# Loading a third block of query weights ahead of a second block of tokens, and spreading the second tokens' layer-norm statistics over ScalarE and VectorE

## The chip, the cores and the metric

The kernel runs on one core of a Trainium2 chip. The metric is device time in microseconds (us) of one execution. Every kernel here was run several times, each time on the same chip next to the kernel before. One execution of each was recorded with the hardware profiler, and its trace is what the readings below come from.

Engines in the profile lines: PE is TensorE's matmuls, PEld its weight loads, DVE is VectorE, ACT is ScalarE, POOL is GpSimd, SP is SyncE. SPq is the queue on which SP issues DMAs. L272 is line 272 of that kernel's source; the lines of the changed kernel are shifted by a few.

## The reference, cut to what matters

A transformer block with adaptive layer norm. Tokens are 2048 x 1024, there are 32 query heads and 4 key/value heads of 128, and attention goes over the last 512 keys.

```python
h = _layernorm(x) * (1 + ca) + sa          # ca, sa from silu(c) @ w_mod
x = x + ga * _A_ref(h, k_cache, v_cache, wq, wo)     # q = h @ wq; softmax attention; @ wo
h = _layernorm(x) * (1 + cb) + sb
x = x + gb * _B_ref(h, w_gate, w_up, w_down)         # SwiGLU feed-forward
```

Only the first layer norm, of the second chunk of 512 tokens (four tiles of 128 tokens, numbered 4 to 7), and the first query projections are touched by the change.

## The kernel before: the parts that matter

A tracker inserts a semaphore wait wherever an operation reads or writes a buffer that another engine has touched. In the traces each engine works through its own operations in the order of emission. This is the second chunk's path from tokens to a matmul operand:

```python
def ln_stats(t):                      # VectorE: two bn_stats halves, one aggregate; POOL: 1/sqrt(var+eps)
    stats(t, t % 2, 0)
    yield
    stats(t, t % 2, 1)
    aggr(t % 8, t % 2)
    yield

def norm_turn(ch, tt):                # VectorE normalises one tile; SP's DMA transposes it into hT
    t = ch * TPC + tt
    norm(t, t % 8, t % 2, half=True)
    T.op(Q_ln[t % 2], lambda: SP.dma_start_transpose(hT[ch % 2][:, :, tt*P:(tt+1)*P], nscf[t % 2]),
         reads=[B_ns4[t % 2]], writes=B_hT[ch % 2])
# later: modulate(...) scales and shifts each of the 8 blocks of hT on VectorE, in place
```

All four transposes name the same eight buffers of `hT` as written, so each waits for the one before to land, and the modulation waits for the last.

The prologue works on the first chunk. Then come attention iterations `i = 1, 2, ...`. In each, PE runs an optional query projection, the scores of iteration i-1, and the product with V (`pv`) of i-2. The relevant emissions of an iteration, before the change:

```python
def pre0(i):
    ...
    if i in (1, 3, 5):
        q_bias_mm(i + 1, i + 3, QB)             # bias of two heads; VectorE copies it out of bank QB
    if i < NQ0 + 1:
        if i % 2 == 0:
            qproj(NQ0 - 1 + i // 2)             # 8 matmuls into bank QB, then VectorE empties the bank
    elif i + 3 < NDI:
        qproj(i + 3)                            # i = 9: projection 12, the first that reads hT[1]
    if i < 5:
        norm_turn(1, i - 1)                     # iterations 1 to 4
    if 1 <= i < 4:
        stats_now(TPC + i)                      # iterations 1 to 3, whole tiles on VectorE
    if i in (7, 8):
        for dt in range(4 * (i - 7), 4 * (i - 7) + 4):
            modulate(hT[1], B_hT[1], dt, 0, 0, B_mode)
```

The statistics of tile 4 are computed on ScalarE at the end of the prologue.

The softmax here doesn't subtract the row's maximum and nothing guards it: scores larger than these inputs give would overflow.

## Time and profile before

| | |
|---|---|
| time, median of the first 3 runs | 1161.9 us (1161.82 to 1164.61) |
| span of the profiled run | 1160.2 us |
| PE busy | 1143.8 us |
| PE busy in 30 to 60 us | 27.2 of 30 us |

The page's first part (per engine: busy us, share of the span, instructions), for the kernel before:

```profile
PE 1143.8 (99%) x7019; PEld 588.7 (51%) x7105; DVE 819.0 (71%) x1641; ACT 530.6 (46%) x741; POOL 68.2 (6%) x136
```

The Trainium skill, "Perfetto Trace Analysis", Identifying the Most-Contended Engine, warns that matmul busy time says little about the distance to the roofline. It is used here for something else: to find where PE stands still. In the stretches of the kernel before (stretch, its length, then for each of PE, PEld, DVE, ACT and POOL the busy us and the instruction count, then granted PE clock, DMA share, GB/s), the third line is nearly full, so what can be won lies before 60 us.

```profile
10.00:15.00 5.00, 4.21 (x47) 3.18 (x46) 2.74 (x9) 1.56 (x4) 0.93 (x3) 0.69 1.09 356
30.00:60.00 30.00, 27.24 (x278) 16.99 (x281) 25.62 (x65) 21.41 (x30) 5.72 (x11) 1.00 0.75 175
60.00:90.00 30.00, 29.69 (x294) 18.66 (x297) 17.97 (x39) 18.84 (x26) 3.14 (x5) 1.00 0.76 164
```

PE's timeline of the kernel before (start, duration, engine, line, operation, count, and in brackets the idle time before it and what released it) shows the gaps:

```profile
31.31 0.81 PE L272 MATMUL ps<-arena 128*128 128x512 bf16 x3 [0.29 <-DVE arena L673]
...
33.74 3.66 PE L272 MATMUL ps<-arena 128*128 128x512 f16 x28 [0.99 <-DVE bq L668]
...
39.77 1.08 PE L272 MATMUL ps<-arena 128*128 128x129 bf16 x16 [0.87 <-DVE arena L821]
...
51.43 12.87 PE L272 MATMUL ps<-arena 128*128 128x512 bf16 x108 [0.24 <-ACT arena L799]
```

(PSUM is the memory that matmuls write to; a bank is a part of it, and it must be emptied before the next matmuls can use it.) The 0.99 us precedes projection 8, whose bank is freed by a bias copy that stands behind eight shifts in VectorE's queue. The 0.87 us precedes the second `pv`, whose banks VectorE empties late because bn_stats stand before that work. Two lines that looked harmless in this profile turn out to matter: POOL's two weight loads, and the last layer-norm transpose on SP's queue shortly after them.

```profile
43.44 1.79 POOL L939 DMA_DIRECT2D arena<-in_A_wo_dram  x2
```

```profile
45.11 1.23 SPq L446 DMA_TRANSPOSE arena<-nsc  x1
```

The 1.23 us is only the issue. The DMA view of the kernel before, asked for 45 to 47 us, gives in its last column the time from issue to landing: 6.2 us, so this transpose landed at about 51.3.

```profile
arena<-nsc SPq DMA_TRANSPOSE x1, 6.2
```

The modulation that reads it, on VectorE, began at 52.39. The transpose had 1.1 us to spare, and nobody waited.

```profile
52.39 1.38 DVE L432 TENSOR_SCALAR arena<-arena,gain,mod_bf 128x512 f16<-128x512 f16 x4
```

The chain that ended last, by engine, in the kernel before:

```profile
PE 95%; DVE 3%; ACT 1%; issue 1%; DMA 1%; SPq 0%; DVEq 0%; ACTq 0%
```

### The profile page before, as it was taken

Reading aid. Unit: us, or ns where it says so; the run is one execution under the profiler, and the core shown is the slowest. Engines: PE = TensorE matmul, PEld = TensorE weight load, DVE = VectorE, ACT = ScalarE, POOL = GpSimd, SP = SyncE. Lnnn points to the kernel's source line nnn. Section 1 sums busy time; section 2 is a strip of 40 time slices with the busy share of each in tenths; the row PEclk is TensorE's granted clock in tenths of the full one; section 3 lists DMA queues with packets and bytes.
Section 4 is the critical chain, followed back from the end, with each engine's and each line's share of the span. In section 5 each row is a group of like instructions: output and inputs, shape, how many; then the busy total and the mean of one; then the engine's idle time right before and its main releaser. Section 6 shows DMA issues by size and latency. Waiting matters only on the chain.

```text
span 1160.2 us, 18184 instructions
## 1 busy us (share of the span) xinstructions
PE 1143.8 (99%) x7019; PEld 588.7 (51%) x7105; DVE 819.0 (71%) x1641; ACT 530.6 (46%) x741; POOL 68.2 (6%) x136
## 2 busy tenths in 40 slices
PE   8999999999999999999999999999999999999999
PEld 5565556554446666566444444444444444444444
DVE  4858997758576777776567898767558777776536
ACT  3766777730117777787110344454110444544110
POOL 1100221000000111111000010000000000000000
PEclk9999999999999999999999999999999999999999
DMA  9779999967906998844765332333764424234443
GB/s 326 170 174 218 221 208 218 211 162 203 248 10 171 193 204 192 213 97 107 193 189 183 76 106 73 101 82 100 208 185 155 123 74 109 73 95 131 131 160 109
DMA packets 289941, 179.98 MB, mean 155 GB/s; under 512 B 130496, under 2 KB 278080, under 8 KB 289856
## 3 DMA queue, kind: packets, MB, share of 16 engines
q1 hardware_dynamic: 226880, 92.31, 36.4%
q10 hardware_dynamic: 54336, 55.05, 14.8%
q0 software_dynamic: 8640, 31.46, 9.3%
q8 instruction: 56, 0.92, 0.3%
q14 instruction: 29, 0.24, 0.1%
HBM read 128.45 MB, written 19.92 MB: 128 GB/s over the span
## 4 chain that ended last, share of the span: by engine, by line
PE 95%; DVE 3%; ACT 1%; issue 1%; DMA 1%; SPq 0%; DVEq 0%; ACTq 0%
PE ps L272 95%; ACT arena L799 1%; DMA arena<-in_A_wq_dram 1%; DVE arena L829 1%; DVE st L413 1%; DVE arena L900 0%; DVE arena L678 0%; SPq L341 0%; DVE arena L673 0%; SPq L310 0%; DVE nsc L427 0%; DVE arena L846 0%; PE ps L276 0%; DVE arena L1544 0%; DVE arena L647 0%
## 5 line engine op out<-in xcount | busy, mean ns | idle before, releaser
L272 PE MATMUL ps<-arena 128*128 128x512 f16 (+2 forms) x6714 | 1135.5, 330 | 12.4 <-POOL arena L406 2.2
L272 PEld LDWEIGHTS ps<-arena 128*128 128x128 bf16 (+1 forms) x6800 | 578.2, 98 | 562.8 <-DVE arena L829 6.2
L799 ACT ACTIVATE arena<-ps 128x1024 bf16<-128x1024 f32 x256 | 261.3, 1021 | 48.4 <-PE ps L272 36.6
L832 ACT ACTIVATE tmp<-ps 128x512 f32<-128x512 f32 x167 | 99.7, 597 | 295.5 <-PE ps L272 282.1
L900 DVE TENSOR_TENSOR arena<-arena 128x512 f16<-128x512 bf16 x328 | 133.4, 419 | 3.0
L829 DVE TENSOR_TENSOR arena<-ps,tmp 128x512 bf16<-128x512 f32 (+1 forms) x134 | 91.9, 686 | 49.7 <-PE ps L272 38.2
L832 ACT ACTIVATE nsc<-ps 128x512 f32<-128x512 f32 x84 | 50.1, 596 | 93.2 <-PE ps L272 90.9
L821 DVE TENSOR_TENSOR arena<-ps,rl 128x512 f16<-128x512 f32 x128 | 88.5, 692 | 4.7 <-DVE rl L818 0.2
L829 DVE TENSOR_TENSOR arena<-ps,nsc 128x512 f16<-128x512 f32 x84 | 57.4, 687 | 40.8 <-PE ps L272 29.6
L818 DVE RECIPROCAL rl<-ps 128x4 f32<-128x4 f32 x128 | 23.1, 180 | 87.8 <-PE ps L272 86.8
L1529 ACT ACTIVATE arena<-arena 128x512 f16<-128x512 f16 x84 | 49.9, 624 | 32.7 <-DVE arena L829 32.7
L1038 DVE TENSOR_TENSOR arena<-arena 128x2048 f16<-128x2048 f16 (+3 forms) x56 | 56.1, 1011 | 9.3 <-PE ps L272 8.8
L1114 DVE TENSOR_TENSOR tmp<-ps,tmp 128x512 f32<-128x512 f32 x32 | 22.1, 690 | 53.1 <-ACT tmp L832 45.3
L832 ACT ACTIVATE arena<-ps 128x512 f32<-128x512 f32 x16 | 9.6, 597 | 90.9 <-PE ps L272 90.9
L950 DVE TENSOR_TENSOR arena<-arena 128x512 f16<-128x512 bf16 x120 | 47.9, 420 | 2.2 <-DMA arena<-in_A_wo_dram 1.2
L413 DVE BATCH_NORM_STATS2 st<-x_res 128x6 f32<-128x512 bf16 x60 | 41.0, 683 | 4.3 <-DMA x_res<-in_A_x_dram 3.9
L427 DVE TENSOR_SCALAR nsc<-x_res,mv,rstd 128x1024 f16<-128x1024 bf16 (+1 forms) x30 | 16.2, 539 | 27.6 <-DMA arena<-nsc 27.6
L1544 DVE TENSOR_TENSOR arena<-arena 128x512 f16<-128x512 f16 x84 | 35.0, 417 | 0.3
L1115 DVE TENSOR_TENSOR tmp<-tmp,rowb 128x512 f32<-128x512 f32 (+1 forms) x49 | 33.6, 686 | 1.7
L594 DVE SCALAR_TENSOR_TENSOR arena<-arena 128x1024 bf16<-128x1024 bf16 x24 | 29.2, 1216 | 0.0
L1116 DVE TENSOR_TENSOR arena<-tmp,x_res 128x512 bf16<-128x512 f32 (+1 forms) x33 | 22.3, 676 | 1.1
L829 DVE TENSOR_TENSOR arena<-ps,rowb 128x512 f16<-128x512 f32 x28 | 19.3, 689 | 3.9 <-ACT rowb L832 3.4
(87 smaller groups left out, 331.5 us busy)
## 6 DMA issues: line engine op xcount, KB each, us to landing
arena<-in_A_wq_dram SPq DMA_DIRECT2D x28, 512.0 KB, 4.9
arena<-wo_sum ACTq DMA_DIRECT2D x7, 2048.0 KB, 9.1
arena<-in_B_w_gate_dram SPq DMA_DIRECT2D x28, 512.0 KB, 4.0
arena<-in_B_w_up_dram SPq DMA_DIRECT2D x28, 512.0 KB, 4.9
arena<-wd_sum ACTq DMA_DIRECT2D x8, 1792.0 KB, 7.9
arena<-in_B_w_down_dram ACTq DMA_DIRECT2D x6, 1792.0 KB, 7.1
arena<-in_A_wo_dram POOLq DMA_DIRECT2D x16, 512.0 KB, 5.0
wo_sum<-arena POOLq DMA_DIRECT2D x16, 512.0 KB, 4.7
```

The costliest lines, as they stand in the source:

```text
L272: T.op(PE, lambda: TE.matmul(out_ap, lhsT, rhs, start=start, stop=stop, skip_group_check=skip), reads=reads, writes=[bank_buf])
L413: T.op(DVE, lambda: V.bn_stats(st_[sl][:, hf * 6:hf * 6 + 6], x_res[:, t, hf * 512:hf * 512 + 512]), reads=[B_x[t]], writes=[B_st[sl]])
L799: T.op(ACT, lambda: A.activation(ex_s[es][:, 2 * kp:2 * kp + 2, :], banks2(SCB + 2 * kp), AF.Exp, scale=att_scale), writes=[PB[SCB + 2 * k ...
L821: T.op(DVE, lambda: V.tensor_tensor(o_s[os_].rearrange("p (a b) d -> p a b d", a=2), psap(PVB * 512, [[512, 2], [130, 2], [1, P]]), rlb, A ...
L829: T.op(DVE, lambda: V.tensor_tensor(out, bank(ba), other, ADD), reads=[ob2], writes=[PB[ba], ob])
L832: T.op(ACT, lambda: A.activation(dst, bank(bk), AF.Copy), writes=[PB[bk], db])
L900: T.op(st, lambda: eng.tensor_tensor(o, a, b, op), reads=rd, writes=[wr])
L950: T.op(DVE, lambda: V.tensor_tensor(o, a, b, SUB), reads=rd, writes=[wr])
L1038: T.op(DVE, lambda: V.tensor_tensor(o, a, b, SUB), reads=rd, writes=[sb])
L1115: T.op(DVE, lambda: V.tensor_tensor(tm, tm, rw, MULT), reads=[B_row[row]], writes=[tb])
L1529: T.op(ACT, lambda: A.activation(o, s_, AF.Silu), reads=[sb], writes=[ob])
L1544: T.op(DVE, lambda: V.tensor_tensor(gu[blk][:, p, :], o, s_, MULT), reads=[sb, ob], writes=[B_gu[blk][p]])
```

## The change

The intent: bring the query weights of projection 8 in before the second tokens; take one more tile's statistics from VectorE, which has no gap from 31.3 to 46.4 us, to ScalarE; cut the rest into half steps, so that no long piece of work delays the emptying of PSUM banks. The normalisations move from iterations 1-4 to 3-6, the modulation from 7-8 to 8-9 and in front of the projection. The diff, cut to its core:

```diff
             load_v(0)
             load_k(1)
+            load_wq(2)
             load_x(1)
-            load_wq(2)
 ...
             def stats_act(t):                    # now a generator in two half steps
-                o, ob = nsc4[t % 2], B_ns4[t % 2]
+                o, ob = tmp[0][:, :].bitcast(BF16), B_tmp[0]
                 T.op(ACT, ... AF.Copy, accum_out=acc[:, 0:1] ...)
                 T.op(POOL, ... mean ...)
+                yield
                 T.op(ACT, ... AF.Square, bias=mean, scale=-1.0, accum_out=acc[:, 1:2] ...)
                 rstd_of(sl, acc[:, 1:2], B_acc, 1.0 / D)
+                yield
 ...
             qproj_mm(7, QB0[7], HK, DT)
-            stats_act(TPC)
             q_raw(7)
 ...
+            x1_stats = [both(stats_act(TPC), stats_act(TPC + 1)), both(ln_stats(TPC + 2), ln_stats(TPC + 3))]
+            NORMS = {3: 0, 4: 2, 5: 1, 6: 3}
 ...
             def pre0(i):
+                if i in (8, 9):
+                    for dt in range(4 * (i - 8), 4 * (i - 8) + 4):
+                        modulate(hT[1], B_hT[1], dt, 0, 0, B_mode)
                 if i < NQ0 + 1:
                     if i % 2 == 0:
                         qproj(NQ0 - 1 + i // 2)
                 elif i + 3 < NDI:
                     qproj(i + 3)
-                if i < 5:
-                    norm_turn(1, i - 1)
-                if 1 <= i < 4:
-                    stats_now(TPC + i)
-                if i in (7, 8):
-                    ... modulate ...
+                if i in NORMS:
+                    norm_turn(1, NORMS[i], i % 2)
+                if 2 <= i < 6:
+                    next(x1_stats[1])
 ...
             def tick0(i):
+                if 1 <= i < 5:
+                    next(x1_stats[0])            # a ScalarE half step behind each exp pair
```

## The prediction

> **What bounds it.** TensorE: the chain that ended last is 95% matmul; the page shows PE busy 1143.8 of 1160.2 us. The change touches the prologue and the first ten attention iterations, 28 to 60 us. The table of stretches gives PE 27.2 of 30 us in 30:60, so at most 2.8 us (0.24%) can be won; 60:90 has 0.3 us idle. PE's gaps in the timeline: 0.29 at 31.3 (VectorE shift of head 0), 0.99 at 33.7 (bias copy, queued behind eight 0.35 us shifts), 0.87 at 39.8 (pv normalisation of iteration 0, queued behind VectorE statistics), 0.24 at 51.4 (ScalarE exp), small ones at 44.7 and 45.3. VectorE has no gap from 31.3 to 46.4.
>
> **What changes.**
> 1. Load order. The second tokens landed at 28.8 and kept ScalarE idle 2.2 us, but no matmul waited for that. The third query weights landed at 31.8 (issue 19.5 plus 12.3); their first matmul ran at 33.7 and waited for VectorE. So the order alone is worth about 0. Tokens will land near 31.5; ScalarE asks for them near 33.8.
> 2. One tile's statistics (1.42 us bn_stats plus aggregate) go from VectorE to ScalarE, which now does two tiles in four half steps, one behind each exp pair of iterations 1 to 4. A half step occupies it 1.15 us (trace: 1.06 and 1.15 us plus a 0.19 us accumulator read, overlapping). The Trainium skill, "ScalarE: Activation LUTs", What ACT_TABLE_LOAD costs, gives 186 ns + 0.833 N (plus 93 ns for a pointer bias): 1.04 and 1.13 us for N = 1024; the trace agrees. No table load is added (instruction order).
> 3. VectorE keeps two tiles, a 0.7 us half in each of iterations 2 to 5; normalisations move from iterations 1-4 to 3-6, modulation of the second chunk from 7-8 to 8-9.
>
> **Critical path, walked by hand with trace durations.** The 0.29 and 0.99 us gaps stay. The 0.87 us gap goes: that normalisation should end near 38.4, not 39.7. New waits: (a) the first normalisation, iteration 3, needs the ScalarE half step that ends near 39.4 plus 1.1 us on POOL, so VectorE idles about 1.3 us near 39.2 to 40.5, and 0.4 us near 46.5; behind it pv waits about 0.5 us near 46. (b) exps come later: ScalarE carries 2.0 + 1.15 us per iteration against 3.3 us of PE. (c) the second half of the modulation (4 x 0.34 us) now stands directly before the projection that reads it, in iteration 9, and behind that iteration's pv normalisation: PE should stop about 0.8 us there (near 58). Sum: -0.9 for the gap, +0.2 to 0.5 for (a) and (b), +0.5 to 1.0 for (c): about 0 to +1 us. After 60 us PE is full, so this stays to the end.
>
> **Predicted**: 1162.5 us (80%: 1160.3 to 1164.6). Faster by over 2%: 0.5%; within 2%: 99%; slower: 0.5%.
>
> **What would show it.** Right: the 0.87 us gap near 39.8 gone; VectorE idle before the norm in iteration 3, released by POOL; no PE wait for query weights in either kernel; a new PE wait released by the modulation near 58; busy PE in 30:60 again 26.5 to 28 us; ScalarE's 2.2 us wait for tokens gone.
>
> **What would make it wrong.** If the transposes of the last normalisation land late (3.7 us median, each waits for the one before), the modulation blocks VectorE and PE by more, +2 us. If the modulation beats the matmuls, the change wins 1 to 1.5 us. If tokens land after 34, everything behind the first half step slips.

## More of the kernel before

After the last of its small `rstd` operations, POOL issues two loads of 512 KB each of the output projection's weights (`unit_load`, first called in iteration 8). Nothing in the program holds them back. They go out as soon as POOL's queue reaches them: in the kernel before that is in iteration 4, four iterations before the place where they stand in the program.

## The result

| | before | changed |
|---|---|---|
| runs | 6 | 6 |
| median | 1163.13 us | 1165.9 us |
| lowest to highest | 1161.82 to 1164.61 | 1164.18 to 1167.36 |
| span of the profiled run | 1160.2 us | 1162.4 us |

The ratio is 1.0023, with a 95% interval of 1.001 to 1.0037. Ratios here are the mean time of one kernel's runs over that of the other's of the same rounds, so not quite the ratio of the medians quoted. The change makes the kernel slower by about 0.2%, or 2.7 us. That is well inside 2%, but 1165.9 us lies above the range of the forecast, and the forecast change was +0.6 us (1162.5 against the 1161.9 then known).

The same stretches of the changed kernel:

```profile
10.00:15.00 5.00, 4.29 (x78) 3.77 (x75) 2.94 (x9) 1.89 (x4) 0.75 (x2) 1.00 1.09 352
30.00:60.00 30.00, 25.00 (x250) 14.99 (x248) 22.53 (x58) 23.03 (x34) 5.69 (x12) 1.00 0.68 173
60.00:90.00 30.00, 30.00 (x297) 18.69 (x297) 17.38 (x38) 18.85 (x25) 2.57 (x4) 1.00 0.65 170
```

The loss is in 30 to 60 us. PE's timeline of the changed kernel there:

```profile
32.23 3.66 PE L272 MATMUL ps<-arena 128*128 128x512 f16 x28 [0.99 <-DVE bq L669]
...
36.35 1.94 PE L272 MATMUL ps<-arena 128*128 128x512 bf16 x20
...
42.35 0.55 PE L272 MATMUL ps<-mod_bf,arena 128*128 128x1 bf16 x16 [0.24 <-DVE arena L648]
...
44.22 5.23 PE L272 MATMUL ps<-arena 128*128 128x129 bf16 x50 [0.43 <-DVE arena L819]
49.69 5.23 PE L272 MATMUL ps<-arena 128*128 128x512 bf16 x50 [0.24 <-ACT arena L797]
57.91 8.41 PE L272 MATMUL ps<-arena 128*128 128x512 f16 x59 [3.00 <-DVE arena L648]
```

The 0.87 us gap before the second `pv` (the product with V) is gone: scores and `pv` now run as one block of 20. In its place stands one gap of 3.00 us that ends at 57.9. Its releaser, L648, is VectorE emptying the bank of projection 11. VectorE's timeline says why it came so late:

```profile
52.06 0.68 DVE L618 CAST arena<-ps 128x512 bf16<-128x512 f32 x1
55.87 1.38 DVE L432 TENSOR_SCALAR arena<-arena,gain,mod_bf 128x512 f16<-128x512 f16 x4 [3.13 <-DMA arena<-nsc]
57.17 0.69 DVE L648 CAST arena<-ps 128x512 bf16<-128x512 f32 x1
```

VectorE stood 3.13 us in front of the modulation, waiting for the last transpose to land. The bank's evacuation stands behind the modulation in the same queue. The transpose, and POOL's weight loads, in the changed kernel's timeline:

```profile
47.59 1.69 POOL L937 DMA_DIRECT2D arena<-in_A_wo_dram  x2
```

```profile
49.45 1.37 SPq L447 DMA_TRANSPOSE arena<-nsc  x1
```

and the DMA view for 49 to 50.5 us:

```profile
arena<-in_A_wo_dram POOLq DMA_DIRECT2D x1, 512.0 KB, 6.3
arena<-nsc SPq DMA_TRANSPOSE x1, 6.4
```

The transpose took 6.4 us to land, although the median of the 28 layer-norm transposes in this profile is 3.4 us. A reader who looks only at SP's line sees 1.37 us. The Trainium skill, "Perfetto Trace Analysis", Per-instruction lifecycle, says that for a DMA instruction the whole data movement falls outside the profiled window, and this line agrees: 1.37 us shown, 6.4 us until the data were there.

What happened meanwhile is in the same view, asked for 49.75 to 53.2 us. By queue, it gives packets, MB and the share of the 16 DMA engines; q0 carries POOL's loads, q1 all that SP issues:

```profile
q0 software_dynamic: 230, 0.87, 71.7%
...
q1 hardware_dynamic: 35, 0.00, 0.6%
```

For 3.4 us almost nothing of the transpose moved, while the loads did. From 53.2 to 56 us, with the loads nearly through, q1 moved 0.55 MB.

The chain that ended last now runs through it. By engine, and the pieces of the chain around 50 us (start, duration, what):

```profile
PE 93%; DMA 3%; DVE 3%; SPq 1%; ACT 1%; issue 1%; POOL 0%; DVEq 0%; ACTq 0%; POOLq 0%
```

```profile
49.05 0.40 DVE arena L819
49.45 6.40 DMA arena<-nsc
55.85 0.03 issue
55.87 0.04 DVE arena L432
```

POOL's loads moved with the change without being touched by it. They follow the last `rstd` operation in POOL's queue. That operation belongs to the last tile's statistics, which are now finished in iteration 5 instead of 3 (tile 7 in both), so the loads went out at 47.6 instead of 43.4 us.

**Theory A.** The two weight loads share the DMA engines with the last transpose and double its landing time. The change has taken away the slack that hid this.

**Rival B.** The transpose is late because it is issued late and stands behind other transposes of its own queue; the loads have nothing to do with it.

Two side questions: does VectorE's queue order add to the wait (A1), or only the data (B1)? And what is the load order alone worth?

One trap must be named first. Up to 31 us the changed kernel's profile is 1.5 us ahead of the first profile of before (the transposes of the second key group start at 30.85 against 32.37 us), and no part of the change does that. The line of 10 to 15 us shows the likely reason: the granted clock was 0.69 in that one execution of the kernel before (half clock from 11.92 to 15.34 us), and 1.00 in every profile taken since. For stage times I therefore use the control e5 below, a second profile of the unaltered kernel. As a yardstick that leaves out the prologue I take the time from the start of those key transposes on PE to the start of VectorE's emptying of projection 12, called "the stretch": 27.62 us in the control (30.87 to 58.49), 29.59 us in the changed kernel (30.85 to 60.44). There is one profile of each kernel here, two of the kernel before. What follows after the stretch took 1101.7 to 1103.0 us in the twelve profiles, whatever the kernel, so the kernels differ in the stretch, and a single span carries about 1 us of noise besides.

### The profile page after: what moved, and what is told of

It is laid out like the page before. It is cut to its first block, busy times and chain, and to the rows that moved or that the text cites. A ratio compares the mean times of both kernels' runs of the same rounds, so it can differ in the third digit from the quotient of the medians. Undisturbed runs are those within 1.5% of the kernel's fastest.

```text
span 1162.4 us, 18269 instructions
## 1 busy us (share of the span) xinstructions
PE 1148.6 (99%) x7105; PEld 587.7 (51%) x7105; DVE 817.8 (70%) x1638; ACT 532.6 (46%) x745; POOL 68.1 (6%) x137
## 4 chain that ended last, share of the span: by engine, by line
PE 93%; DMA 3%; DVE 3%; SPq 1%; ACT 1%; issue 1%; POOL 0%; DVEq 0%; ACTq 0%; POOLq 0%
PE ps L272 92%; DMA arena<-in_A_wq_dram 1%; DMA arena<-in_A_wo_dram 1%; DVE arena L827 1%; DMA arena<-nsc 1%; SPq L341 0%; DVE arena L898 0%; DMA wo_sum<-arena 0%; ACT arena L797 0%; DVE arena L819 0%; DVE st L413 0%; DVE arena L679 0%; SPq L310 0%; DVE arena L432 0%; DVE arena L674 0%
## 5 line engine op out<-in xcount | busy, mean ns | idle before, releaser
L432 DVE TENSOR_SCALAR arena<-arena,gain,mod_bf 128x512 f16<-128x512 f16 x56 | 20.3, 409 | 3.1 <-DMA arena<-nsc 3.1
```

## The experiments

All ten kernels gave correct results. The ratio is always against the kernel before in the same rounds.

### e1: hold the two weight loads until the modulation has begun

```diff
-  T.op(Q_of[slot][0], lambda: g.dma_start(dst, src), writes=[w.b_raw, w.b_s3])
+  T.op(Q_of[slot][0], lambda: g.dma_start(dst, src), reads=[B_hT[1][3]] if k < 2 else [], writes=[w.b_raw, w.b_s3])
```

> Changed kernel; only the first two output-weight loads (2 x 512 KB, issued by POOL at 47.6 us in the changed kernel) are held until the fourth modulation of the second chunk has run. Theory A (these loads share the DMA engines with the last normalisation's transpose and make it land 6.4 us after issue): that transpose lands in 3.0 to 3.8 us, VectorE's 3.1 us wait for it falls to 0 to 0.5 us, PE's 3.0 us wait near 55 falls below 1 us; time 2 to 3.5 us below the changed kernel. Rival B (the transpose is late because it is issued late and stands behind other transposes of its own queue): landing stays above 5.5 us, PE wait stays at 2.5 to 3 us, same time as the changed kernel.

Measured: median 1161.69 us (1161.42 to 1162.34), ratio 0.9988 (0.9974 to 1.0003). The loads went out at 54.9 us, after the modulation. The DMA view for the last transpose, issued at 49.78:

```profile
arena<-nsc SPq DMA_TRANSPOSE x1, 3.4
```

VectorE no longer waits for the transpose, and the longest PE wait near 56 us is 0.5 us, released by the modulation itself. The stretch is 26.95 us. Theory A's landing and waits came in; rival B's did not. The time came out lower than theory A said: 4.1 us below the changed kernel by the two ratios, where 2 to 3.5 were expected. The transpose was issued at the same point of its queue and behind the same transposes as before, and only the loads were gone.

### e2: empty the bank before the modulation in iteration 8

```diff
-  if i in (8, 9):
+  if i == 9:
       for dt in range(4 * (i - 8), 4 * (i - 8) + 4): modulate(...)
   ... qproj ...
+  if i == 8:
+      for dt in range(4 * (i - 8), 4 * (i - 8) + 4): modulate(...)
```

> Changed kernel; in iteration 8 the modulation stands behind the evacuation of projection 11 again, as in the kernel before (iteration 9 unchanged). Theory A1 (PE's 3.0 us wait is made of the late transpose AND of VectorE's in-order queue: the PSUM evacuation that frees the bank is stuck behind the modulation that waits): the late landing stays (6 us), VectorE still waits about 2.5 us for it, but PE's wait is 0.5 to 1.5 us shorter. Rival B1 (only the data matter: the projection needs the modulated tokens anyhow): PE's wait within 0.4 us of 3.0.

Measured: median 1164.92 us, ratio 1.002 (1.0003 to 1.0036). The landing was 6.9 us beside the loads, and VectorE waited 2.6 us. PE's one wait became two, 2.01 and 0.65 us, both released by the modulation; the sum of 2.66 is 0.34 less than before. By the line drawn beforehand (within 0.4) that is B1: the releaser named by the profile, the stuck evacuation, is real, but taking it away uncovers the wait for the data behind it, since projection 12 needs the modulated tokens anyhow. But it is not settled. Measured from the start of PE's wait, the transpose landed 0.5 us later here than in the changed kernel (56.13 against 54.65 us, and 55.85 against 54.91). With the same landing the sum would be about 2.1 us, an estimate from these numbers, and that lies in A1's range. The evacuation's part is somewhere between 0.3 and 0.8 us; the greater part of the wait is for the data. The profile of this run also shows a half-speed clock from 57.8 us, between the two waits; see below.

### e3: issue the two weight loads early, in iteration 1

```diff
 def tick0(i):
     if 1 <= i < 5:
         next(x1_stats[0])
+    if i == 1:
+        chain[0] = unit_chain(0, HP)
+        next(chain[0])                 # issues both loads, near 34 us
 ...
-    if i == 8:
-        chain[0] = unit_chain(0, HP)
-    if 8 <= i < NI - 8:
+    if 9 <= i < NI - 8:
         unit_tick(i)
```

> Changed kernel; the same two loads are issued earlier, in iteration 1 (near 34 us, where the DMA engines stand nearly idle, 31 GB/s in 35:40) instead of near 47.6 us. Theory A: the last transpose lands in 3.0 to 3.8 us, PE's 3.0 us wait is gone or below 1 us, time 2 to 3.5 us below the changed kernel and 0 to 1.5 us below the kernel before. Rival B: landing above 5.5 us, same time as the changed kernel.

Measured: median 1161.79 us (1160.81 to 1165.16), ratio 0.9994 (0.997 to 1.0017). The loads went out at 33.9 us. The last transpose, issued at 49.69:

```profile
arena<-nsc SPq DMA_TRANSPOSE x1, 3.1
```

PE's waits in 28 to 66 us that are not also in the changed kernel come to a single 0.2 us at the modulation. The loads now lie beside the first of the four transposes, which took 3.7 us instead of 3.2 and delayed nobody. PE busy in 30 to 60 us is 27.82 us, against 25.00 in the changed kernel and 26.35 in the control. The stretch is 26.80 us. So with the loads out of the way the change does what it was meant to do: 0.8 us less than the control. The time itself, about 1 us below before by the medians, is not clear of the noise; three of the four runs lie between 1160.8 and 1162.4 us, the fourth at 1165.2.

### e4: the kernel before, with only the modulation moved

```diff
-  if i in (7, 8): ... modulate ...                 # behind the projection
+  if i in (8, 9): ... modulate ...                 # in front of the projection, as in the changed kernel
```

> Kernel before; only the modulation is moved, to iterations 8 and 9, in front of the projection, as in the changed kernel. The transposes landed by 51.3 us there, so VectorE should not wait for them. My forecast's term (c): a PE wait of 0.5 to 0.9 us in the projection of iteration 9, time 0.5 to 0.9 us above the kernel before. Rival (the modulation position alone costs nothing, only the late landing costs): PE wait below 0.3 us, same time within 0.5 us.

Measured: median 1163.17 us, ratio 1.0001 (0.9986 to 1.0016). There is no wait for the transpose, and PE waits 0.46 us for the modulation in front of projection 12. The stretch is 27.82 us, 0.2 more than the control. The 0.46 us lies between the two forecasts (0.5 to 0.9 us for term (c), below 0.3 for the rival). The place of the modulation alone costs a few tenths and is not visible in the time. It is not what made the changed kernel slow.

### e5: the kernel before, unaltered, as a control

> The kernel before, unaltered: a control. Ratio 1.000 within 0.0015, which tells how small a difference these rounds can show. Second question: the profile of before that the forecast was read from had a granted clock of 0.69 in 10:15 us and reached the attention 1.5 us later than all runs since. Theory C: at full clock in the prologue the first projection of the third query weights waits for its DMA (about 1.2 us released by the query weights, instead of 0.99 us released by VectorE), and the pv gap near 39 is 1.2 to 1.5 us instead of 0.87. Rival: the same 0.99 and 0.87 us as in the first profile.

Measured: median 1163.06 us, ratio 1.0009 (0.9993 to 1.0025). The interval reaches 0.16% to either side, so smaller differences can't be told from nothing in three rounds. PE's timeline of this second profile of before, at full clock in the prologue:

```profile
32.61 2.33 PE L272 MATMUL ps<-arena 128*128 128x512 f16 x10 [1.36 <-DMA arena<-in_A_wq_dram]
...
39.84 1.08 PE L272 MATMUL ps<-arena 128*128 128x129 bf16 x16 [1.37 <-DVE arena L821]
```

Theory C holds. When the prologue is not slowed, projection 8 does wait for the query weights, and the `pv` gap is 1.37 instead of 0.87 us. The stretch is 27.62 us, against 26.05 us in the first profile (32.37 to 58.42): the 1.5 us that the first execution had lost in its prologue all came back here. The loads did not come earlier with PE: the third query weights were issued at 20.23 us and landed 12.3 us later, near 32.5 us, against 31.8 in the first profile. The later PE comes, the less it waits for them. The intent of the change was right about something that my profile could not show.

### e6: the kernel before, with only the load order changed

```diff
-            load_x(1)
             load_wq(2)
+            load_x(1)
```

> Kernel before; only the load order is changed (third query weights ahead of the second tokens). My forecast: worth 0. Theory C: the wait for the query weights (about 1.2 us) becomes the 0.99 us wait for VectorE, but the tokens land 2 to 3 us later, and VectorE, which in this kernel needs them in iteration 1, waits: pv gap and later gaps grow by 1 to 3 us, so the order pays only together with the later statistics. Rival: time and waits unchanged within 0.3 us.

Measured: median 1166.29 us, ratio 1.0028 (1.0015 to 1.0041), 3.3 us slower. The wait for the weights became the 0.99 us wait for VectorE, as expected. But ScalarE now waits 7.4 us for the tokens (4.5 in the control) with its statistics of tile 4, which stand before the first exps, and PE then waits 2.60 us for the exps. Theory C had the loss in another place, behind VectorE: the `pv` gap did not grow but shrank to 0.66 us. The order alone is harmful. It may pay only with the later statistics that come with it in the change (e7).

### e7: the changed kernel, with only the load order put back

> Changed kernel; only the load order is put back (second tokens first). Theory A (the loss is the late transpose alone): PE's wait near 55 stays at 2.5 to 3.5 us, landing above 5.5 us, time within 0.6 us of the changed kernel, with a wait for the query weights of 0.2 to 0.5 us more at projection 8. Rival (the order causes the loss by delaying the tokens): the 3 us wait shrinks to below 1.5 us.

Measured: median 1167.09 us, ratio 1.0036 (1.0023 to 1.0049). The transpose lands in 7.1 us, and PE waits 3.65 us near 60, a little more than the 2.5 to 3.5 expected: the order does not cause the loss, and theory A stands. Projection 8 now waits 1.50 us for the query weights instead of 0.99. The time missed the expectation of 0.6 us: it is 1.2 us above the changed kernel by the medians of two sessions, and the intervals of the two ratios overlap, so the difference is not clear of noise. The stretches of the profiled run show what may lie behind it (the granted clock is the third number from the right):

```profile
32.00:36.00 4.00, 3.54 (x9) 1.30 (x10) 0.66 (x2) 1.12 (x3) 0.23 (x1) 0.57 0.11 26
36.00:40.00 4.00, 3.92 (x60) 3.00 (x59) 2.96 (x7) 3.42 (x5) 0.16 (x1) 1.00 0.01 4
58.00:60.00 2.00, 0.00 (x0) 0.00 (x0) 1.56 (x5) 0.00 (x0) 0.00 (x0) 0.94 1.10 370
60.00:62.00 2.00, 1.52 (x4) 0.58 (x5) 1.97 (x6) 0.00 (x0) 0.00 (x0) 0.50 1.09 349
```

After each of the two gaps the granted clock falls to about half. The 28 matmuls of projection 8, scores and `pv` took 5.33 us where they take 3.66 us in the changed kernel: 1.67 us more.

### The second price of a gap: the clock gate

The Trainium skill, "TensorE: Matmul & The Clock Gate", Part 1, says that the PE clock is gated to half after an idle window of about 3.4 us, that the window runs freely, and that a busy window of the same length releases it. The traces agree in kind: half clock (0.50 to 0.57 in the stretches) stands after the 2.01 us gap of e2, the 2.60 us gap of e6 and both gaps of e7. It does not stand after the 3.00 us gap in the profile of the changed kernel, whose clock is 1.00 throughout 30 to 60 us. The gaps of 1.50, 2.01 and 2.60 us are shorter than the 3.4 us of the page.

Where a gap falls goes far to explain which ones are hit. By the clock records of these traces, each half-clock stretch inside a kernel lasted 3.41 us, and all began on a grid with a step of 3.41 us that does not start with the kernel. The same view for cells of that grid: two cells each of e2 (2.01 us gap), of e7 (1.50 us gap) and of the changed kernel (3.00 us gap). The first number after the length is PE busy.

```profile
54.38:57.79 3.41, 1.40 (x9) 0.47 (x6) 1.57 (x6) 1.02 (x1) 0.00 (x0) 1.00 0.99 284
57.79:61.20 3.41, 2.76 (x7) 0.87 (x7) 2.39 (x6) 0.00 (x0) 0.00 (x0) 0.50 1.14 285
```

```profile
29.03:32.45 3.42, 1.64 (x24) 1.02 (x24) 3.38 (x13) 3.01 (x4) 0.00 (x0) 1.00 1.06 286
32.45:35.86 3.41, 3.40 (x9) 1.20 (x10) 0.21 (x1) 0.67 (x2) 0.23 (x1) 0.50 0.06 15
```

```profile
53.07:56.49 3.42, 1.85 (x21) 1.20 (x19) 0.62 (x2) 2.05 (x2) 0.00 (x0) 1.00 1.19 268
56.49:59.90 3.41, 1.89 (x7) 0.60 (x7) 3.38 (x10) 0.00 (x0) 0.00 (x0) 1.00 1.07 365
```

The gaps of e2 and e7 lie within one cell, and the next cell runs at half clock. The longer gap of the changed kernel, like the 2.44 us gap of e8 below, is split between two cells, and the clock stays. Over all cells of the twelve profiles from the first clock record on (5 to 8 us), the four with PE busy for 1.64 us or less were followed by half clock. Of the cells with 1.84 us or more only one was, in the prologue of the first profile of before (2.29 us), so busy time is not the whole rule.

The mean granted clock that each run records shows how often some half clock occurred. Rounded to three places, it is below 1.000 in 5 of 6 runs of the changed kernel, 4 of 4 of e2, 4 of 4 of e6 and 3 of 4 of e7, all kernels with a gap of 2 us or more in their profile. It is so in 2 of 6 runs of e8, whose profile has such a gap too, in 0 of 4 runs of e1 and 0 of 5 of e10, in 1 of 4 of e3, e4 and e9, in 2 of 4 of the control e5, and in 8 of 27 runs of the kernel before beside the experiments. The mean does not say where in the run it was. My estimate from these numbers: the stretch says 1.97 us of loss, and the remaining 0.7 us of the measured 2.7 us is about what 1.67 us in a good part of the runs would give. That sum is rough: the single runs were not traced, and single spans carry about 1 us of other noise.

### e8: early weight loads, and the bias product in another bank

```diff
-                    q_bias_mm(i + 1, i + 3, QB)
+                    q_bias_mm(i + 1, i + 3, PVB + 1 if i == 1 else QB)
```
(on top of e3)

> Changed kernel with the two early output-weight loads of e3, and the bias product of heads 2 and 3 put into another PSUM bank, so that projection 8 no longer waits for the copy of that bias queued behind eight shifts. Expected: landing 3 to 3.5 us, PE's wait near 55 gone as in e3, the 0.99 us wait at projection 8 falls below 0.4 us; 0.6 to 1.0 us below e3 and 1 to 2.5 us below the kernel before (ratio 0.998 to 0.999). Rival: the time saved at projection 8 is lost again at the next wait for VectorE (pv gap grows by as much), time as e3.

Measured: median 1161.8 us (1160.1 to 1163.45), ratio 0.9991 (0.9978 to 1.0004). The 0.99 us wait at projection 8 is gone altogether. But in the profiled run the third transpose took 5.0 us to land with no weight load beside it; the fourth, which must wait for it, was issued only at 51.22, and VectorE again waited 2.57 us and PE 2.44 us near 56. Three of the six runs lie at 1160.1 to 1160.7 us and three at 1162.9 to 1163.5, which fits a transpose that is late in some runs and not in others. The DMA view of that run shows that most of its data had moved by 49.6 us and that a rest trickled in at about 10 GB/s until 51; what slowed it I could not settle. The result says that the chain of four transposes, each waiting for the one before, has no slack left in this schedule.

### e9: the kernel before, with early weight loads

The same edit as in e3, on the kernel before.

> Kernel before; the two output-weight loads are issued in iteration 1, as in e3. Theory A says that the kernel before has the same collision (its last transpose, issued 45.1 us, took 6.2 us beside loads issued at 43.4) but had time for it: the landing should fall to 3 to 4 us and the time stay the same (ratio 0.999 to 1.001), since no matmul waited. Rival (early loads are a gain in themselves, so e3 proves nothing about the change): 1.5 to 3 us below the kernel before.

Measured: median 1162.26 us, ratio 0.9997 (0.9982 to 1.0013). The last transpose, issued at 47.32, lands in 3.2 us instead of 6.2, and the time is the same. So the kernel before had the same collision, and it cost nothing there because the modulation came late enough. The collision did not vanish but moved: the loads went out at 36.63 us, and the second transpose, now beside them, took 6.6 us (3.7 in the control). This is theory A on another transpose. Early loads are not a gain in themselves.

### e10: give the slack back

On top of e3: the other bank of e8, the order of e2, and the VectorE tiles first.

```diff
-            NORMS = {3: 0, 4: 2, 5: 1, 6: 3}
+            NORMS = {3: 2, 4: 0, 5: 3, 6: 1}
 ...
-                if 2 <= i < 6:
+                if 1 <= i < 5:
                     next(x1_stats[1])
```

> Changed kernel with early output-weight loads (e3), the bias product in another bank (e8), the modulation of iteration 8 behind the projection's evacuation (e2), and the VectorE tiles normalised first (their statistics one iteration earlier), so that no normalisation waits for ScalarE and POOL. Expected: VectorE's 1.2 and 0.5 us waits for POOL gone, first transpose about 1 us earlier, no PE wait above 0.6 us between 31 and 60 us, all or nearly all runs at granted clock 1.000, time 1159.5 to 1161.5 us, ratio 0.997 to 0.999. Rival (e8's late transpose was not for want of slack): some runs again 2.5 us slower than the fastest, ratio 0.999 to 1.000.

Measured: median 1160.6 us (1159.86 to 1161.87), ratio 0.9983 (0.9971 to 0.9996). This is below both kernels: about 2 us below the kernel before, with an interval clear of 1 (though far inside 2%), and about 4.7 us below the changed kernel, each by the medians of its own rounds. All five runs have a granted clock of 1.000. PE's timeline has no gap above 0.6 us between 31 and 60 us:

```profile
31.41 3.66 PE L272 MATMUL ps<-arena 128*128 128x512 f16 x28
...
48.77 6.10 PE L272 MATMUL ps<-arena 128*128 128x512 bf16 x54 [0.51 <-ACT arena L797]
55.45 10.77 PE L272 MATMUL ps<-arena 128*128 128x512 f16 x81 [0.58 <-DVE arena L432]
```

VectorE's waits for POOL are gone, the last transpose was issued at 48.60 and landed in 3.5 us (the first, beside the early loads, took 4.4), and the stretch is 25.65 us, 1.97 below the control. Which of the three additions gave how much was not measured one by one. The largest single wait left is 0.58 us at the modulation; the ScalarE exps are next.

The experiments side by side:

| kernel | last transpose, issue to landing | longest PE wait, 50 to 61 us | stretch | ratio |
|---|---|---|---|---|
| e5, control | 6.3 us | 0.24 us | 27.62 us | 1.0009 |
| changed | 6.4 us | 3.00 us | 29.59 us | 1.0023 |
| e1, loads held | 3.4 us | 0.5 us | 26.95 us | 0.9988 |
| e2, bank emptied first | 6.9 us | 2.01 us | 30.11 us | 1.0020 |
| e3, loads early | 3.1 us | 0.20 us | 26.80 us | 0.9994 |
| e4, before with late modulation | 6.3 us | 0.46 us | 27.82 us | 1.0001 |
| e6, before with new order | 6.3 us | 0.24 us | 30.34 us | 1.0028 |
| e7, changed with old order | 7.1 us | 3.65 us | 33.15 us | 1.0036 |
| e8, early and bank | 3.2 us (third: 5.0) | 2.44 us | 28.15 us | 0.9991 |
| e9, before with early loads | 3.2 us | 0.24 us | 27.36 us | 0.9997 |
| e10, early and slack | 3.5 us | 0.58 us | 25.65 us | 0.9983 |

The stretches of e2, e6 and e7 contain half-clock time; that of e6 also its 2.60 us wait near 36.

## Why the prediction was wrong

What held. The 0.87 us gap went. VectorE waits for POOL before the first normalisation (1.18 us measured, "about 1.3" forecast) and again in iteration 5 (0.47, "0.4"). `pv` waits 0.43 us behind it ("about 0.5"). The 0.24 us wait for an exp, near 49.7, is not a new cost: the kernel before has the same at 51.4. A wait of 0.24 us for VectorE at 42.35 is new, so (a) and (b) together came to 0.67 us, where 0.2 to 0.5 were forecast. PE does stop in the projection of iteration 9, for the modulation. A ScalarE half step took 1.05 and 1.14 us, as the trace of before had it.

The step that failed is term (c), "PE should stop about 0.8 us there". It was 3.00 us, because VectorE stood 3.13 us waiting for the last transpose. I computed the term from VectorE's queue alone and let the transpose land in the median time. The last transpose was not a median one even in the profile that I had: it took 6.2 us, and one question to the DMA view would have said so. I also took POOL's loads for fixed in time, though nothing holds them but POOL's own queue, into which the change moved later work. And I did not compare the two moves. The normalisations went back by two iterations, the modulation by only one: the last transpose was issued 4.3 us later than in the control (49.45 against 45.18), but VectorE was ready for the modulation only 0.3 us later (52.74 against 52.45). So "+2 us" stood among the things that would make the forecast wrong, with the right cause in outline, and I gave it too little weight. My walk also had PE reach this place later than it did, near 58, when it was there at 54.9 (1.5 us of this is the slowed prologue of the profile I walked from), and that, as I read it, made the wait look shorter.

"The order alone is worth about 0" is wrong as well. Alone it costs 3.3 us (e6). Inside the change it removes 0.5 us of wait at projection 8 in the profiles (1.50 against 0.99 us, e7 against the changed kernel). I read it from one profile with a slowed prologue, in which the weights happened to be in time. The second tokens also landed later than forecast: they were issued at 20.3 and took 12.6 us, so 32.9 us instead of 31.5, which left ScalarE a wait of 0.57 us.

Two smaller misses. PE busy in 30 to 60 us was to be 26.5 to 28 and was 25.00. And the level: I took the 1161.9 us of three runs for the kernel before; over six runs its median was 1163.13, so some 1.2 us of the miss in absolute time is not the change.

In short: without the collision the change is worth about -0.8 us (e3's stretch against the control), the collision adds 2.8 us to the stretch (29.59 against 26.80), and by my estimate the clock gate adds some 0.7 us on the mean of the runs.

## What to carry to other kernels

When work moves to another engine, look at what stands behind it in that engine's queue: DMA issues that nothing else holds back go out when the queue reaches them, so moving small operations moves large transfers. For every transfer that will be nearer to its reader after a change, read its own issue-to-landing time and its slack, not the median of its group. A wait of 2 to 3 us on TensorE may cost more than its length, because the clock can drop to half after it, depending on where it falls; and one profile of the kernel before is one execution, so take a second before reading gaps of a few tenths.

## What the Trainium skill lacked or had wrong

- "DMA: Bandwidth & Descriptors", Rules for kernel authors, says that a transpose next to ordinary DMAs needs nothing. For correctness no run contradicts it (all results were correct), but it lacks the time: the last layer-norm transpose landed in 3.1 to 3.5 us alone (e1, e3, e10) and in 6.2 to 7.1 us beside two 512 KB loads (before, changed, e2, e7). The section Issuing engines are not separate DMA queues, which says that DMAs from all engines share the same 16 DMA engines and interleave, agrees as to the sharing. Of interleaving the changed kernel shows little: for 3.4 us POOL's queue moved 0.87 MB and SP's 0.00.
- "TensorE: Matmul & The Clock Gate", Part 1, gives an idle window of about 3.4 us. Here half clock followed gaps of 1.50 us (e7), 2.01 us (e2) and 2.60 us (e6), and did not follow one of 3.00 us (changed kernel). The page's free-running window agrees with the 3.41 us grid of these traces. It lacks how much idle time within one window is enough: here half clock followed the cells in which PE was busy for 1.64 us or less, and, in the attention stretch, none with 1.84 us or more (one in the prologue, with 2.29 us, was).
- No page explains why a transpose without a large load beside it can take 5.0 us (e8, third transpose).
